# Attention and two mixture layers on one core: gate logits cut into queued pieces, and second products of the small experts without a summing product

## Chip, core and metric

The kernel runs on one core of a Trainium2 chip. TensorE multiplies matrices into PSUM; VectorE (DVE), ScalarE (ACT) and GpSimd (POOL) do the element-wise work; SyncE (SP) issues most of the transfers. The metric is the device time of one execution in microseconds (us). All data is 32-bit floating point; TensorE takes it as pairs of words (`float32r`, high and low part, three products for one) up to the first expert, and as plain `float32` in the small experts, where one product of the program is two matmul records of the trace.

## The reference

```python
def reference(q, k, v, w_in, w_out, w_skip, w_gate, w1, w2):
    x = block_causal_attention(q, k, v)          # 4 x 8 heads x 576 x 64 -> 2304 tokens x 512
    h = x @ w_in                                 # 512 -> 2048
    x = np.maximum(0.01 * h, h) @ w_out          # leaky maximum, 2048 -> 512
    do_compute = x @ w_skip > 0                  # tokens that go to an expert
    xc = x[do_compute]
    logits = xc @ w_gate                         # 8 experts
    e_idx, gate_w = argmax(logits), softmax(logits)[argmax]
    for e in range(8):
        m = e_idx == e
        y[m] = gate_w[m] * (relu(xc[m] @ w1[e]) @ w2[e])     # 512 -> 1024 -> 512
    out = x; out[do_compute] = xc + y
```

## The kernel before

The program is traced in Python; a scheduler fixes the order of the instructions on every engine at build time. It takes an instruction when its inputs are ready by its own reckoning, earlier traced ones first. `tc.keep_in_program_order` (`pin`) holds an instruction of an engine to the traced order. `tc.issue_after(ins)` makes the instructions traced inside it that run on the engine of `ins` come after `ins` in that engine's queue.

**Attention** and a quarter of the leaky layer take the first 315 us. **The main loop** (L1088 to L1123) does the rest of the leaky layer: 384 tokens `n` at a time, 72 passes `i`, in each a first product `b_mm1` (12 matmuls of 384 columns into `ph`, one of two PSUM banks) and, for the pass two earlier, a second product `b_mm2` (9 matmuls of 512 columns into `acc`). Between the two stands `leaky`: ACT scales `ph` into `u`, DVE takes the maximum of `ph` and `u` (L517), ACT casts it to `gh`, POOL subtracts to `gl` (L518). The bank of `ph` is free when DVE's maximum has read it. Tokens come in the order 3, 4, 5 (four inner blocks each, three times over), then 0, 1, 2 (twelve each). When the last block of an `n` is summed, L902 adds three times on DVE, and the routing steps of this `n` go into a list `rq` from which each pass takes one, from pass 60 on two. They are `keep` (stores), three of `logits` (one for 128 tokens), `route`, `place_all` (the row of each token in the lists) and `put` (three indirect transfers from POOL's queue, L847). For `n` = 3, 4, 5 and 0, `logits` multiplies on DVE: for each of nine rows `wrow` one instruction multiplies 128 x 512 numbers and sums them (L748), and a short one reads the sum. For `n` = 1 the logits are TensorE's (`logits_last`); 2 comes behind the loop. In pass 67 the lists are read back (`load_lists(lf)`, L713), and `gather(first)` (L717) fetches the first expert's tokens; after pass 71 TensorE turns them (`turn_x`, L989).

**The sorted experts** come last. Expert 0's tiles run at full precision; the other seven experts are sorted by their count of tokens, and the tail (L1427 to L1445) computes seven units: three `Groups` units of 96 tokens, two of 32, a `Half` of 64 and a `Full` of 128, the last two for one expert. A unit has `first` and `rest` (first product and ReLU on ACT), `turn` (transposes, then a DVE copy into `hT`, L1275), `second` (second product) and `end`. In pass `i` of the tail TensorE's pinned order is `first` of the next unit, `turn`, `rest` of the next, `end` of the one before, `turn_x` two units on, `second`. A group of `m` = 32 tokens fills a quarter of TensorE's columns, so four products with their own weights run side by side and write four quarters of a bank `pp`: in `second_product` (L1277) each quarter takes another quarter of the 1024 inner rows, so the bank holds four partial sums of one 32 x 512 result. ACT or DVE copies the bank to `ev` (L1394, for `Half` L1358), and `end` multiplies `ev` with `sums`, a matrix of ones that adds the quarters (L1399; `Half`, with two halves, L1362). `end_tile` multiplies by the gate and adds the input on DVE (L1291) and scatters the rows (L1292). Weights arrive expert by expert from `load_rank` on SP's queue, each into the place of one that is done.

Of the kernel before, what the change touches and what calls it, by code (L numbers as in the profile page):

```python
# [10 lines left out]
F32 = mybir.dt.float32  # L11
# [5 lines left out]
ALU = mybir.AluOpType  # L17
AX = mybir.AxisListType
# [379 lines left out]
def attention_moe_kernel(  # L398
# [13 lines left out]
    nc = tc.nc  # L412
    B, H, S, HD = q.shape
    NT, D = out.shape
# [6 lines left out]
    E, _, F2 = w1.shape  # L421
    ND = D // 128
    NF2 = F2 // 128
    TB = 3
# [7 lines left out]
    ident = C.tile([128, 128], F32, name="ident")  # L432
# [6 lines left out]
    CV = ctx.enter_context(tc.tile_pool(name="cv", bufs=2))  # L439
# [192 lines left out]
    psx = ctx.enter_context(tc.tile_pool(name="psx", bufs=1, space=PSUM))  # L632
# [51 lines left out]
    def load_rows():  # L684

        for j, nm in ((0, "raw"), (2, "raw"), (4, "raw"), (6, "cv2"), (7, "cv2"), (8, "cv2")):
            n = 2 if nm == "raw" else 1
            t = CV.tile([128, n, D], F32, name=nm, bufs=3)
            nc.sync.dma_start(t, wr_d[j : j + n].unsqueeze(0).to_broadcast([128, n, D]))
            wrow.extend(t[:, k_] for k_ in range(n))  # L690
# [34 lines left out]
    def routing_steps(n, x2):  # L725
        box = {}
        last, late = n == order[-1], n in order[-2:]
# [3 lines left out]
        pin = tc.keep_in_program_order if last else lambda ins: ins  # L731
# [7 lines left out]
                nc.sync.dma_start(x2_d[pos * 128 : (pos + TB) * 128].rearrange("(t p) d -> p t d", p=128), x2)  # L739
            tc.keep_in_program_order(nc.sync.dma_start(out[rows].rearrange("(t p) d -> p t d", p=128), x2))  # L740

        def logits(t):

            if t == 0:
                box["L"] = s3("lg", 1 + E)
            for j in range(1 + E):
                junk = M2.tile([128, D], F32, name="xlast", bufs=3)
                nc.vector.tensor_tensor_reduce(out=junk, in0=x2[:, t], in1=wrow[j], scale=1.0, scalar=0.0,  # L748
                                               op0=ALU.mult, op1=ALU.add, accum_out=box["L"][:, t, j : j + 1])
# [100 lines left out]

        if last:
            return dict(keep=keep, turn=turn_last, mul=mul_last, route=route, rank=rank, place=place_all, put=put)
        return [keep] + [lambda t=t: (logits_last if late else logits)(t) for t in range(TB)] + [route, place_all, put]

    parts = {}

# [18 lines left out]
    def b_mm1(n, f):  # L875
        if f == 0 and n not in parts:
            load_part(n)
        ph = ps2.tile([128, 512], F32, name="ph2", bufs=2)[:, 0:BT]
        o = (n % 3) * BT
        three(ph, [(wi_b[0](c, f), wi_b[1](c, f)) for c in range(ND)],  # L880
              [(xT[0][:, c, o : o + BT], xT[1][:, c, o : o + BT]) for c in range(ND)], True, True)
        gh = M2.tile([128, BT], F32R, name="gh", bufs=2)
        gl = M2.tile([128, BT], F32R, name="gl", bufs=2)
        ends = leaky(M2, ph, BT, gh, gl, 2)
        gq[n, f] = (gh, gl)
        if f == NFB - 1 and n >= 3:
            load_x(n - 3)
        return ends
# [198 lines left out]
    rq = []  # L1087
    for i in range(len(seq) + lag):  # L1088
        gate[:] = ends if i else a_ends
        if wb and i % 3 < 2:  # L1090
            wb.pop(0)()
            if not wb:
                gate.clear()
                load_rows()
        if i < len(seq):
            ends = b_mm1(*seq[i])
        for _ in range(1 if i < len(seq) - NFB else 2):
            if rq:
                rq.pop(0)()
        f = i - (len(seq) - NFB)  # L1100
        if f == 3:
            for j in range(AHEAD):
                if tags[j]:
                    load_piece(j)
        if 4 <= f < 8:
            run_all(w_steps(f - 3))
        if f == 7:

            load_lists(lf, lambda l: l[0:256, :].rearrange("(n p) c -> p n c", p=128), nc.sync)
            find(lf, 0, 1)  # L1110
            gather(first, NT - BT)
        if f == NFB - 1:
            with ExitStack() as behind:
                for ins in ends:
                    behind.enter_context(tc.issue_after(ins.ins))
                run_all(w_steps(8))
        if i >= lag:
            n, f = seq[i - lag]
            add = b_mm2(n, f)
            if f == NFB - 1 and n != order[-1]:  # L1120
                rq += routing_steps(n, parts[n])
        if i == len(seq):
            turn_x(first, psx.tile([128, ND, 128], F32, name="py", bufs=1), False)  # L1123
# [27 lines left out]
    MG, MH = 32, 64  # L1151
# [44 lines left out]
    _, rank = nc.values_load_multi_w_load_instructions(tab[0:1, 0:NR, 0], engines=[mybir.EngineType.SP], min_val=1, max_val=NR)  # L1196
# [46 lines left out]
    M3 = ctx.enter_context(tc.tile_pool(name="m3", bufs=2))  # L1243
# [6 lines left out]
    pin = tc.keep_in_program_order  # L1250
    bank = lambda nm: ps3.tile([128, 512], F32, name=nm, tag="ps")
# [24 lines left out]

    def second_product(pp, w, h, m):  # L1277

        s = 128 // m
        n = NF2 // s  # L1280
        for i in range(n):
            for j in range(s):
                pin(nc.tensor.matmul(pp[j * m : j * m + m], h[:, i * 128 + j * m : i * 128 + j * m + m], w[1][j * n + i], start=(i == 0), stop=(i == n - 1)))  # L1283

    def end_tile(y, lx, n=128):
        yo = M3.tile([128, 512], F32, name="yo")
        y = y if isinstance(y, list) else [y]
        w = D // len(y)
        for k_, t in enumerate(y):
            c = slice(k_ * w, k_ * w + w)  # L1290
            nc.vector.scalar_tensor_tensor(out=yo[0:n, c], in0=t[0:n], scalar=lx["li"][0:n, 2:3], in1=lx["xg"][0:n, c], op0=ALU.mult, op1=ALU.add)  # L1291
        nc.gpsimd.indirect_dma_start(out=out[:, :], out_offset=bass.IndirectOffsetOnAxis(ap=lx["ix"][0:n, 1:2], axis=0),  # L1292
                                     in_=yo[0:n], in_offset=None, bounds_check=NT - 1, oob_is_err=False)

# [19 lines left out]
    class Full(Unit):  # L1314
# [17 lines left out]
        def second(self):  # L1332
            self.y = [bank("py")[:, 0:256] for _ in range(2)]
            for k_ in range(2):
                for f in range(NF2):
                    pin(nc.tensor.matmul(self.y[k_], hT[:, f // 4, f % 4 * 128 : f % 4 * 128 + 128], self.w[1][f][:, k_ * 256 : k_ * 256 + 256],
                                         start=(f == 0), stop=(f == NF2 - 1)))

        def end(self):
            end_tile(self.y, self.lx, self.n)  # L1340

    class Half(Unit):

# [11 lines left out]
        def second(self):  # L1355
            pp = bank("pp")
            second_product(pp, self.w, hT[:, 0], MH)
            nc.scalar.copy(ev[0], pp)  # L1358

        def end(self):  # L1360
            y = psx.tile([128, 512], F32, name="py", bufs=1)
            pin(nc.tensor.matmul(y[0:MH], sums[MH], ev[0], start=True, stop=True))  # L1362
            end_tile(y, self.lx, MH)

    class Groups(Unit):

# [21 lines left out]
                turn_groups(h2[a // 2], hT[:, a // 2], 2 * min(2, self.n // MG - a))  # L1388

        def second(self):  # L1390
            for g in range(self.n // MG):
                pp = bank("pp")
                second_product(pp, self.w, hT[:, g // 2, g % 2 * 256 : g % 2 * 256 + 256], MG)
                (nc.vector.tensor_copy if g % 2 else nc.scalar.copy)(ev[g], pp)  # L1394

        def end(self):
            y = psx.tile([128, 512], F32, name="py", bufs=1)
            for g in range(self.n // MG):
                pin(nc.tensor.matmul(y[g * MG : g * MG + MG], sums[MG], ev[g], start=True, stop=True))  # L1399
            end_tile(y, self.lx, self.n)  # L1400

    units = [Groups(r - 1, r, r, CAPS[r]) for r in range(1, 6)] + [Half(5, 0, NR, MH), Full(6, 0, 0, 128)]
    U = len(units)
# [13 lines left out]
        held[r] = load_rank(r)  # L1417

    h2 = [CV.tile([128, 512], F32, name="cv3", bufs=3) for _ in range(2)]
    hT, ev01, ev23 = (CV.tile([128, 2, 512], F32, name="raw", bufs=3) for _ in range(3))  # L1420
    ev = [ev01[:, 0], ev01[:, 1], ev23[:, 0], ev23[:, 1]]
    hx = CV.tile([128, 512], F32, name="cv2", bufs=3)
    sums = {m: M3.tile([128, m], F32, name=f"sum{m}", bufs=1) for m in (MG, MH)}
    for m, t in sums.items():
        nc.vector.reduce_sum(out=t, in_=ident.rearrange("p (s t) -> p t s", t=m), axis=AX.X)

    units[0].first()  # L1427
    units[0].rest()
# [26 lines left out]
    lx = lane32(llate, 0, xgs[4], xws[2])  # L1455
    to = held[places_of[3]]
    w = split(to)

    def half(row):
        load_lists(part, lambda l: l[bass.ds(row, MH), :].unsqueeze(1), nc.sync)  # L1460
        find(part)
        gather_n(lx, MH)
        turn_n(lx, MH)
        ph = bank("ph3")
        first_product(ph, w, lx["xw"][:, :, 0:MH], MH)
        relu(hx, ph)
        turn_groups(hx, hT[:, 1])
        pp = bank("pp")
        second_product(pp, w, hT[:, 1], MH)
        nc.scalar.copy(hx, pp)  # L1470
        y = bank("py")
        pin(nc.tensor.matmul(y[0:MH], sums[MH], hx, start=True, stop=True))
        end_tile(y, lx, MH)

    with tc.If(spill > 0):
        with tc.For_i(0, E, 1) as r:
# [36 lines left out]
```

## Time and profile before

| | us |
|---|---|
| three runs | 764.28, 765.04, 766.53 |
| median | 765.04 |
| the profiled execution | 765.64 |
| its span, first to last instruction | 763.8 |
| TensorE busy in it | 730.6 (96%) |
| DVE, ACT, POOL busy | 460.4, 354.9, 319.2 |
| mean granted clock of TensorE | 0.994 of 2.4 GHz |

Times in the rows are microseconds from the start of the span, unless they are marked ns; the profiled execution is 1.84 us longer than its span. A busy TensorE is not TensorE at its peak. L12 is line 12 of the kernel; names are those of its tiles, without numbers. PEld is TensorE's loading of weights, SPq and POOLq the queues of engines that issue transfers.

### The profile page before, as it was taken

To read this page: it belongs to the slowest core of one execution; us is meant where nothing else is said; L and a number is where in the kernel's file an instruction comes from. 1 tells how busy PE (TensorE), PEld (TensorE's weight loads), DVE (VectorE), ACT (ScalarE), POOL (GpSimd) and SP (SyncE) were. 2 spreads that over 40 slices of the span, in tenths; PEclk is the share of its full clock that TensorE was granted. 3 is DMA by queue.
4 is the path that set the end of the run, shared out by engine and by line. 5 is a ranking of instruction groups with operands and counts; after the bars stand their busy time and mean duration, and the time that the engine had idled before them with its cause. 6 is when DMAs were issued, how large, how long until landed. Compare 5 with 4: busy or idle time off the path is not lost.

```text
span 763.8 us, 12641 instructions
## 1 busy us (share of the span) xinstructions
PE 730.6 (96%) x4454; PEld 593.1 (78%) x4455; DVE 460.4 (60%) x1067; ACT 354.9 (46%) x824; POOL 319.2 (42%) x429
## 2 busy tenths in 40 slices
PE   5999899999999999999999999999999998999995
PEld 4666778788888788899999998879899976875333
DVE  5888887764668646666773499988821365221211
ACT  4786887775788746555452222222223251222110
POOL 4656683454335436454442342545431543210111
PEclk9999999999999999999999999999999999999998
DMA  8545644522330214732223457112302221999900
GB/s 183 136 116 133 181 103 113 144 65 73 90 77 17 95 58 148 272 100 81 98 83 111 123 150 251 56 43 84 125 0 83 57 96 32 301 399 397 353 25 24
DMA packets 101109, 96.92 MB, mean 127 GB/s; under 512 B 69198, under 2 KB 72270, under 8 KB 101042
## 3 DMA queue, kind: packets, MB, share of 16 engines
q1 hardware_dynamic: 92578, 82.28, 34.5%
q0 software_dynamic: 7264, 13.50, 6.1%
q8 instruction: 36, 0.59, 0.3%
q10 hardware_dynamic: 1200, 0.30, 0.2%
q14 instruction: 31, 0.25, 0.1%
HBM read 74.38 MB, written 21.98 MB: 126 GB/s over the span
## 4 chain that ended last, share of the span: by engine, by line
PE 64%; DVE 21%; ACT 7%; DMA 3%; issue 2%; POOL 1%; SPq 0%; POOLq 0%; ACTq 0%; DVEq 0%
PE ph L526 18%; PE acc L526 12%; DVE xlast L748 9%; PE pv L345 4%; PE po L526 3%; PE ph L1269 3%; PE pp L1283 3%; PE pt L288 3%; PE py L1004 2%; PE sp L229 2%; PE ph L1004 2%; ACT P L193 2%; PE sp L182 2%; DVE stat L192 2%; PE big L110 1%
## 5 line engine op out<-in xcount | busy, mean ns | idle before, releaser
L526 PE MATMUL ph<-xT,wbt 128*128 128x384 f32 x864 | 167.2, 338 | 3.9 <-DVE u L517 2.1
L526 PEld LDWEIGHTS ph<-xT,wbt 128*128 128x128 f32 x864 | 151.8, 188 | 13.5 <-DVE u L517 3.9
L518 POOL TENSOR_TENSOR gl<-u,gh 128x384 fp32r<-128x384 f32 x72 | 80.5, 1119 | 144.5 <-ACT gh L517 140.8
L526 PE MATMUL acc<-wbt,gh 128*128 128x512 f32 x432 | 132.2, 393 | 0.0
L201 POOL TENSOR_SCALAR P<-P,stat 128x256 f32<-128x256 f32 (+4 forms) x144 | 80.0, 573 | 89.5 <-DVE stat L199 73.3
L517 ACT CAST gh<-u 128x384 fp32r<-128x384 f32 x72 | 37.0, 514 | 121.2 <-DVE u L517 49.6
L526 PEld LDWEIGHTS acc<-wbt,gh 128*128 128x128 f32 x432 | 79.7, 188 | 12.0
L517 DVE TENSOR_TENSOR u<-ph,u 128x384 f32<-128x384 f32 x72 | 39.7, 551 | 71.4 <-ACT u L516 71.3
L526 PE MATMUL acc<-wbt,gl 128*128 128x512 f32 x216 | 82.2, 395 | 0.0
L516 ACT ACTIVATE u<-ph 128x384 f32<-128x384 f32 x72 | 35.3, 490 | 61.3 <-PE ph L526 58.2
L288 PE MATMUL pt<-ident,P 128*128 128x128 f32 x400 | 58.2, 275 | 4.4 <-ACT P L193 1.8
L192 DVE TENSOR_REDUCE stat<-sp 128x1 f32<-128x384 f32 (+7 forms) x88 | 45.9, 527 | 25.1 <-PE sp L229 12.8
L288 PEld LDWEIGHTS pt<-ident,P 128*128 128x128 f32 x400 | 47.0, 140 | 16.5 <-ACT P L193 5.4
L193 ACT ACTIVATE P<-sp,stat 128x384 f32<-128x384 f32 (+7 forms) x88 | 49.8, 567 | 20.2 <-DVE stat L192 18.6
L526 PE MATMUL ph<-xT,wia 128*128 128x384 f32 x288 | 57.6, 344 | 0.6 <-ACT xT L350 0.5
L473 POOL TENSOR_TENSOR cv<-cv,cv 128x512 int32<-128x512 int32 x32 | 43.7, 1366 | 33.7 <-DVE cv L472 26.9
L526 PE MATMUL po<-woa,gA 128*128 128x512 f32 x216 | 55.4, 399 | 0.0
L748 DVE CUSTOM_DVE_ANT_0 xlast<-x,raw 128x512 f32<-128x512 f32 x72 | 55.1, 804 | 0.0
L526 PEld LDWEIGHTS ph<-xT,wia 128*128 128x128 f32 x288 | 49.4, 188 | 2.3 <-ACT xT L350 0.7
L345 PE MATMUL pv<-ph,vn 128*64 128x320 f32 (+4 forms) x448 | 49.6, 370 | 0.4 <-ACT P L242 0.3
L526 PEld LDWEIGHTS acc<-wbt,gl 128*128 128x128 f32 x216 | 40.4, 188 | 8.5
L345 PEld LDWEIGHTS pv<-ph,vn 128*64 128x64 f32 x448 | 30.3, 140 | 20.8 <-issue 2.8
(282 smaller groups left out, 1249.6 us busy)
## 6 DMA issues: line engine op xcount, KB each, us to landing
wbt<-in_moe_w_dram SPq DMA_DIRECT2D x40, 512.0 KB
raw<-in_moe_w_in_dram SPq DMA_DIRECT2D x16, 512.0 KB
raw<-in_moe_w_out_dram SPq DMA_DIRECT2D x16, 512.0 KB
xTd<-xT POOLq DMA_DIRECT2D x4, 1152.0 KB
part_d<-cv SPq DMA_DIRECT2D x18, 256.0 KB
x<-part_d SPq DMA_DIRECT2D x6, 768.0 KB
xT<-xTd POOLq DMA_DIRECT2D x6, 768.0 KB
out_dram<-x SPq DMA_DIRECT2D x6, 768.0 KB
```

The lines of the kernel that those rows point to most:

```text
L192: self.recent["max"] = nc.vector.tensor_reduce(out=st_[:, 1, i : i + 1], in_=sv, op=ALU.max, axis=ax, negate=True)
L193: self.recent["exp"] = nc.scalar.activation(out=P, in_=sv, func=AF.Exp, bias=st_[:, 1, i : i + 1], accum_out=st_[:, 0, i : i + 1])
L201: nc.gpsimd.tensor_scalar(out=P, in0=P, scalar1=rs[:, i : i + 1], scalar2=1.0, op0=ALU.mult, op1=ALU.mult)
L288: nc.tensor.transpose(o, src, self.ident)
L345: self.pin(nc.tensor.matmul(box["pv"][64 * h : 64 * h + 64, c0:N], st()["vs"][:, jc, h], box["ph"][:, i, h, cs], start=(jc == 0), stop=(jc ...
L473: nc.gpsimd.tensor_tensor(out=w, in0=w, in1=low, op=ALU.add)
L516: nc.scalar.activation(out=u, in_=ph, func=AF.Copy, scale=0.01)
L517: return [nc.vector.tensor_tensor(out=u, in0=ph, in1=u, op=ALU.max), nc.scalar.copy(gh, u), nc.gpsimd.tensor_tensor(out=gl, in0=u, in1=gh. ...
L518: nc.gpsimd.tensor_tensor(out=gl, in0=u, in1=gh.bitcast(F32), op=ALU.subtract)]
L526: nc.tensor.matmul(ps, x, y, start=first and m == 0, stop=last and m == 3 * n - 1)
L748: nc.vector.tensor_tensor_reduce(out=junk, in0=x2[:, t], in1=wrow[j], scale=1.0, scalar=0.0, op0=ALU.mult, op1=ALU.add, accum_out=box["L"] ...
L1004: nc.tensor.matmul(ps, x, y, start=(i == 0), stop=(i == len(l) - 1))) for i, (x, y) in enumerate(l)]
```

## The change

Two edits. In the main loop, the logits of 128 tokens are two steps of `rq` (five rows of `wrow`, then four); `keep` is no step of its own for these `n` but opens the first piece, so seven steps become nine; and every step's instructions on DVE are queued behind the leaky maximum of the same pass. In the tail, a group's four quarters take other work: two of them the left 256 columns of the result, two the right, each over half of the inner rows (with `m` = 64: one half of the columns each, over all rows). DVE multiplies each quarter by the gate and adds it to the output tile straight from PSUM (`add_groups`), in `second`; the copies to `ev`, the products with ones, `ev` and `sums` go, and `end` only scatters. The same edit is made in a path for spilled tokens.

```diff
-        def logits(t):
-            if t == 0:
+        def logits(t, js):
+            if t == 0 and js[0] == 0:
+                keep()
                 box["L"] = s3("lg", 1 + E)
-            for j in range(1 + E):
+            for j in js:
...
-        return [keep] + [lambda t=t: (logits_last if late else logits)(t) for t in range(TB)] + [route, place_all, put]
+        if late:
+            turns = [keep] + [lambda t=t: logits_last(t) for t in range(TB)]
+        else:
+            turns = [lambda t=t, js=js: logits(t, js) for t in range(TB) for js in (range(0, 5), range(5, 1 + E))]
+        return turns + [route, place_all, put]
...
             if rq:
-                rq.pop(0)()
+                with tc.issue_after(ends[0].ins):
+                    rq.pop(0)()
...
     def second_product(pp, w, h, m):
         s = 128 // m
         n = NF2 // s
-        for i in range(n):
+        for i in range(2 * NF2 // s):
             for j in range(s):
-                pin(nc.tensor.matmul(pp[j * m : j * m + m], h[:, i * 128 + j * m : i * 128 + j * m + m], w[1][j * n + i], start=(i == 0), stop=(i == n - 1)))
-
-    def end_tile(y, lx, n=128):
-        yo = M3.tile([128, 512], F32, name="yo")
-        y = y if isinstance(y, list) else [y]
-        w = D // len(y)
-        for k_, t in enumerate(y):
-            c = slice(k_ * w, k_ * w + w)
-            nc.vector.scalar_tensor_tensor(out=yo[0:n, c], in0=t[0:n], scalar=lx["li"][0:n, 2:3], in1=lx["xg"][0:n, c], op0=ALU.mult, op1=ALU.add)
+                f = j // 2 * 4 + i
+                c, d = f % n * 128 + f // n * m, j % 2 * 256
+                pin(nc.tensor.matmul(pp[j * m : j * m + m, 0:256], h[:, c : c + m], w[1][f][:, d : d + 256], start=(i == 0), stop=(i == 2 * NF2 // s - 1)))
+
+    def add_groups(yo, pp, lx, t0, m):
+        r = slice(t0, t0 + m)
+        for j in range(128 // m):
+            c = slice(j % 2 * 256, j % 2 * 256 + 256)
+            nc.vector.scalar_tensor_tensor(out=yo[r, c], in0=pp[j * m : j * m + m, 0:256], scalar=lx["li"][r, 2:3], in1=(lx["xg"], yo)[j // 2][r, c], op0=ALU.mult, op1=ALU.add)
...
     class Half(Unit):
...
             second_product(pp, self.w, hT[:, 0], MH)
-            nc.scalar.copy(ev[0], pp)
+            self.yo = out_tile()
+            add_groups(self.yo, pp, self.lx, 0, MH)
 
         def end(self):
-            y = psx.tile([128, 512], F32, name="py", bufs=1)
-            pin(nc.tensor.matmul(y[0:MH], sums[MH], ev[0], start=True, stop=True))
-            end_tile(y, self.lx, MH)
+            end_tile(self.yo, self.lx, MH)
 
     class Groups(Unit):
...
         def second(self):
+            self.yo = out_tile()
             for g in range(self.n // MG):
                 pp = bank("pp")
                 second_product(pp, self.w, hT[:, g // 2, g % 2 * 256 : g % 2 * 256 + 256], MG)
-                (nc.vector.tensor_copy if g % 2 else nc.scalar.copy)(ev[g], pp)
+                add_groups(self.yo, pp, self.lx, g * MG, MG)
 
         def end(self):
-            y = psx.tile([128, 512], F32, name="py", bufs=1)
-            for g in range(self.n // MG):
-                pin(nc.tensor.matmul(y[g * MG : g * MG + MG], sums[MG], ev[g], start=True, stop=True))
-            end_tile(y, self.lx, self.n)
+            end_tile(self.yo, self.lx, self.n)
...
-    hT, ev01, ev23 = (CV.tile([128, 2, 512], F32, name="raw", bufs=3) for _ in range(3))
-    ev = [ev01[:, 0], ev01[:, 1], ev23[:, 0], ev23[:, 1]]
+    hT = CV.tile([128, 2, 512], F32, name="raw", bufs=3)
     hx = CV.tile([128, 512], F32, name="cv2", bufs=3)
-    sums = {m: M3.tile([128, m], F32, name=f"sum{m}", bufs=1) for m in (MG, MH)}
-    for m, t in sums.items():
-        nc.vector.reduce_sum(out=t, in_=ident.rearrange("p (s t) -> p t s", t=m), axis=AX.X)
```

## Rows read from the trace of the kernel before

**Rows 1.** Chain that ended last, main loop: start, us, what.

```profile
424.35 2.08 PE ph L526 x12
426.43 2.08 PE acc L526 x9
```

**Rows 2.** Windows: length, busy PE, PEld, DVE, ACT, POOL; clock, DMA share, GB/s.

```profile
432.60:549.36 116.76, 114.19 (x599) 101.23 (x598) 109.73 (x325) 26.12 (x58) 48.39 (x49) 1.00 0.38 122
499.32:507.66 8.34, 7.07 (x34) 5.57 (x32) 8.34 (x27) 0.91 (x2) 1.64 (x2) 1.00 0.00 0
```

**Rows 3.** Groups by line, 428 to 552 us: busy, mean ns | idle before, releaser.

```profile
L526 PE MATMUL ph<-xT,wbt 128*128 128x384 f32 x345 | 66.9, 339 | 2.5 <-DVE u L517 2.1 <-issue 0.4
...
L748 DVE CUSTOM_DVE_ANT_0 xlast<-x,raw 128x512 f32<-128x512 f32 x72 | 55.1, 804 | 0.0
...
L748 DVE CUSTOM_DVE_ANT_0 xlast<-x,cv 128x512 f32<-128x512 f32 x36 | 25.2, 723 | 0.0
...
L517 DVE TENSOR_TENSOR u<-ph,u 128x384 f32<-128x384 f32 x28 | 15.3, 546 | 6.6 <-ACT u L516 6.6
```

**Rows 4.** Timeline of DVE, two neighbouring logits.

```profile
444.35 0.68 DVE L748 CUSTOM_DVE_ANT_0 xlast<-x,raw 128x512 f32<-128x512 f32 x1
...
444.96 0.68 DVE L748 CUSTOM_DVE_ANT_0 xlast<-x,raw 128x512 f32<-128x512 f32 x1
```

**Rows 5.** Timeline from the lists to the first expert's turned tokens.

```profile
609.69 1.03 POOL L717 DMA_INDIRECT xgf<-x_d,lfix  x1 [1.10 <-DVE lfix L708]
...
617.32 0.27 PE L989 MATMUL py<-ident,xgf 128*128 128x128 f32 x1
...
623.10 0.68 DVE L995 TENSOR_TENSOR xtf<-py,xtf 128x512 fp32r<-128x512 f32 x1
```

**Rows 6.** Chain that ended last: a gather's wait, then the tail.

```profile
638.28 3.27 DMA xgf<-x_d,lfix
...
690.46 3.59 PE ph L1269 x64
...
707.15 5.29 PE pp L1283 x48
712.44 0.86 PE ph L1269 x16
713.30 0.81 PE pt L1274 x6
714.11 1.00 PE ph L1269 x16
715.11 0.85 PE py L1399 x6
715.96 0.36 PE pt L1259 x4
...
741.96 0.98 PE py L1399 x2
742.93 3.58 PE pp L1283 x16
746.52 1.02 PE pt L1274 x8
747.54 1.00 PE py L1362 x2
748.54 7.12 PE py L1336 x32
```

**Rows 7.** Groups by line and form, 676 to 764 us.

```profile
L1291 DVE SCALAR_TENSOR_TENSOR yo<-py,rankli,xg 128x256 f32<-128x256 f32 x2 | 1.0, 484 | 5.9 <-PE py L1336 5.9
...
L1291 DVE SCALAR_TENSOR_TENSOR yo<-py,rankli,xg 32x512 f32<-32x512 f32 x1 | 0.7, 737 | 3.7 <-PE py L1399 3.7
```

**Rows 8.** Timeline of DVE in the tail: copies into `hT`.

```profile
713.93 1.02 DVE L1275 COPY raw<-pt 128x512 f32<-128x512 f32 x2 [2.44 <-PE pt L1274]
...
747.14 1.29 DVE L1275 COPY raw<-pt 128x512 f32<-128x512 f32 x2 [3.43 <-PE pt L1274]
```

More of the change, by code (lines that the diff above doesn't have):

```diff
@@ L1280, in second_product, with end_tile @@
         n = NF2 // s
-        for i in range(n):
+        for i in range(2 * NF2 // s):
             for j in range(s):
-                pin(nc.tensor.matmul(pp[j * m : j * m + m], h[:, i * 128 + j * m : i * 128 + j * m + m], w[1][j * n + i], start=(i == 0), stop=(i == n - 1)))
-    def end_tile(y, lx, n=128):
-        yo = M3.tile([128, 512], F32, name="yo")
-        y = y if isinstance(y, list) else [y]
-        w = D // len(y)
-        for k_, t in enumerate(y):
-            c = slice(k_ * w, k_ * w + w)
-            nc.vector.scalar_tensor_tensor(out=yo[0:n, c], in0=t[0:n], scalar=lx["li"][0:n, 2:3], in1=lx["xg"][0:n, c], op0=ALU.mult, op1=ALU.add)
+                f = j // 2 * 4 + i
[6 more added lines that the diff above has]
+            nc.vector.scalar_tensor_tensor(out=yo[r, c], in0=pp[j * m : j * m + m, 0:256], scalar=lx["li"][r, 2:3], in1=(lx["xg"], yo)[j // 2][r, c], op0=ALU.mult, op1=ALU.add)
+    out_tile = lambda: M3.tile([128, 512], F32, name="yo")
+    def end_tile(yo, lx, n=128):
         nc.gpsimd.indirect_dma_start(out=out[:, :], out_offset=bass.IndirectOffsetOnAxis(ap=lx["ix"][0:n, 1:2], axis=0),
@@ L1339, in end @@
         def end(self):
-            end_tile(self.y, self.lx, self.n)
+            yo, lx = out_tile(), self.lx
+            for k_, y in enumerate(self.y):
+                c = slice(k_ * 256, k_ * 256 + 256)
+                nc.vector.scalar_tensor_tensor(out=yo[:, c], in0=y, scalar=lx["li"][:, 2:3], in1=lx["xg"][:, c], op0=ALU.mult, op1=ALU.add)
+            end_tile(yo, lx)
     class Half(Unit):
@@ L1469, in half @@
         second_product(pp, w, hT[:, 1], MH)
[L1470 to L1473, printed above, removed]
+        yo = out_tile()
+        add_groups(yo, pp, lx, 0, MH)
+        end_tile(yo, lx, MH)
     with tc.If(spill > 0):
```

## The prediction

> **What bounds the kernel now.** I read the page first. TensorE is busy nearly throughout, so a change pays where it takes work off TensorE or ends one of its few stalls. The chain of work that ended last says where that is. In the main loop it is nothing but passes of two equal parts, 12 matmuls of `b_mm1` in 2.08 us and 9 of `b_mm2` in 2.08: 4.16 us a pass [rows 1]. In the tail it is TensorE's records without a gap, up to the last product [rows 6]; no transfer and no other engine stands in it. So the tail's length is the sum of TensorE's records.
>
> For the stretch of the logits I took windows. From 432.6 to 549.4 us, 28 passes, DVE is busy 109.7 of 116.8 us and TensorE 114.2: it idles 2.57 us, half of it (1.27) in one window in which DVE never rests [rows 2]. The groups by line name the reason: `b_mm1` waited 2.5 us, 2.1 of it for DVE's maximum in `u` [rows 3]. That is all the main loop can give.
>
> **The logits in pieces.** One of the 108 logits comes 0.61 us after the other [rows 4]. Their mean busy times of 804 and 723 ns against 680 of an undisturbed one [rows 3, 4] add (0.124 x 72 + 0.043 x 36) = 10.5 us of stretching over 28 passes, 0.4 a pass. A pass with nine logits therefore asks of DVE 9 x 0.61 + 0.55 (the maximum [rows 3]) + 0.4 = 6.4 us and lasts 4.16. The bank of `ph` is wanted again three parts later, after 6.25 us; less ACT's and DVE's half microsecond each, a maximum may come some 5.1 us late. Nine logits in front of it (5.5 to 5.9 us) are too many by under a microsecond, which is the size of the stalls.
>
> After the change a pass asks 5 x 0.61 + 0.55 + 0.4 = 4.0 us or 4 x 0.61 + 0.95 = 3.4: both fit a pass, and no maximum stands behind more than five logits. Nine steps for seven spread the work of `n` = 3, 4, 5, 0 over passes 30 to 62 instead of 30 to 57: DVE's 109.7 us and five more maxima, 112.5, in 137 us, 82% against 94%. The logits are not shortened; their cover is the passes that follow, in which DVE has room.
>
> Two places can take some back. From pass 60 two steps are popped a pass, so pass 60 gets nine logits again, and 61 four and the routing: DVE is 2.3 us late after the one and, by my estimate, 3.5 after the other, inside 5.1, but the order on its queue may put a maximum last. And `n` = 1 starts one pass later, so `put`, POOL's three indirect transfers, the lists on SP's queue and `gather(first)` behind them move by 4.16 us. That gather was issued at 609.69; one like it took 3.27 us, so it landed near 612.96, and TensorE turned its tokens at 617.32 [rows 5, 6]: 4.36 us of room, 0.2 of it left. If it is late, the next link is DVE's `xtf`, which began only at 623.10 behind other work [rows 5], so the first microsecond or so is still hidden. `keep`, now in the first piece, puts its stores on SP's queue in the same pass as before for `n` = 3; behind them stand loads that are wanted passes later. I take a gain of the 2.57 us less 0.5: **2.0**, with bounds of 2.6 gained and 2 lost.
>
> **The second products.** Removed from TensorE: three sums of 0.85 us (one is shown), two of 0.98, one of 1.00 [rows 6]: 5.51 us, all on the chain.
>
> Added: matmuls half as wide and twice as many. The narrow form stands in the same trace, in the first products: 64 records of 256 columns in 3.59 us, 56.1 ns each; 48 of 512 columns took 5.29, 110.2 each [rows 6]. A group's second product goes from 16 x 110.2 = 1.76 us to 32 x 56.1 = 1.80. Shorter runs of the narrow form took 0.86 and 1.00 us for 16 [rows 6], 53.8 to 62.5 ns, which bounds a group between 1.72 and 2.00. I take the long run, being the same form at the same length: 11 groups x 0.03 = 0.4 us lost (bounds 0.4 gained, 2.6 lost). `Half`'s 3.58 us becomes 32 records, two side by side; at 7.12 / 32 for a 256-column record [rows 6] that is 3.56: nothing.
>
> The Trainium skill speaks against this part: "TensorE: Matmul & The Clock Gate", section "Wait — 56ns, not 53.3ns?", has the sequencer spend some 62 ns on a matmul when hardware decode is off, and bind where the array needs less. By it the 352 narrow records would take 21.8 us instead of 19.7, and the sum would be 2.1 us worse. The 56.1 ns of the long run lie under that figure.
>
> Moved to DVE: 46 adds of 256 columns instead of copies on ACT and DVE and six wide adds. A 256-column add took 0.484 us; 32 rows save nothing against 128 (0.737 for 32 x 512) [rows 7]. Neighbours on DVE can overlap by 0.07, as logits of 0.68 us do that come 0.61 apart [rows 4]. Four adds of a group so take between 1.73 and 1.94 us, beside TensorE's 1.80: DVE just keeps up and ends some 2 us behind TensorE. Queued behind them are the copies into `hT` for the next unit. The tightest place is the first 32-token neighbour: after a second product TensorE has 0.86 + 0.81 + 1.00 + 0.36 = 3.03 us of other records before the next one [rows 6], and the sum of 0.85 no longer pads it. DVE needs about 2.0 for adds and 1.02 for the copies [rows 8]: 3.0. I price a wait of 0.15 in all (bounds 0 and 0.4). Without those pads the copies are next in line.
>
> Under the last sum the cover goes for certain. `Full`'s second product began 2.02 us after `Half`'s ended: 1.02 of transposes and 1.00 of sum [rows 6], and the copies ended at 748.43 [rows 8], just before. Now `Half`'s two adds (0.9 us) stand before the copies (1.29), so the product starts 1.5 to 2.3 us after `Half`'s. I take 2.0: that 1.00 is not won (bounds 0.5 won, 0.3 lost). ACT's copies and the making of `sums` were beside TensorE's work and cost nothing before or after.
>
> Sum of this part: 5.51 - 0.4 - 1.0 - 0.15 = **4.0 us** gained, bounds 1.2 and 5.5.
>
> **Sum.** The profiled execution took 765.64 us; 765.64 - 2.0 - 4.0 = 759.6. The median of the runs lies 0.6 below it, so I forecast **759.0**.
>
> **Rivals.**
> *The stalls stay* (0.12): the order on DVE's queue is fixed at build time, and the stalls move to passes 60 to 62 or to the adds L902 instead of ending. For it: DVE is still 82% busy. Time: 765.0 - 4.0 = 761.0.
> *DVE sets the tail's pace* (0.12): if a 256-column add costs what a 512-column one does, 0.737, a 96-token unit asks 12 x 0.737 + 1.02 = 9.9 us of DVE, and TensorE's round there, 9.17 from second product to second product [rows 6], is 8.3 without the sum. Two such rounds lose 1.5 each: 762.1. It begins at 0.61 an add. Against it: the 0.484. "TensorEngine Tiling" of the Trainium skill, section on the PSUM bottleneck, warns of this very thing and wants both ScalarE and VectorE to empty PSUM; the change leaves it to VectorE.
> *Narrow records at 62.5 ns* (0.05): 11 groups lose 0.24 instead of 0.03: 761.3. Against it: the run of 64.
> *The first gather is two passes late* (0.05): 8.3 - 4.36 = 4.0 us of waiting at 617: 763.0, no change that can be told.
> *Slower* (0.06): the third and fourth add of a group read what the first and second wrote, and all of them read one quarter of the partitions and may write another, which no row shows. If each waits for the one before and costs two, 0.97, a round asks 12.7 us against 8.3: 8.8 lost in the two rounds, 767.8. It decides from 0.95 an add.
>
> **How the numbers follow.** The forecast has 0.60, with a range of its own from 757.4 to 761.0. I call 0.3% (2.3 us, so 762.7) what a measurement can tell. Faster: 0.60 + 0.12 + 0.12 + 0.05, less 0.04 for those whose spread reaches over 762.7: 0.85. Within: 0.04 + 0.05 = 0.09. Slower: 0.06. The range takes in the first three rivals and, below, both parts near their upper bounds: 756.8 to 762.8; it leaves out the last two and some 0.05 at the lower end.
>
> **What would show it.** Right: no wait of `b_mm1` for `u` between 432 and 550 us and at most 0.5 near passes 60 to 62; TensorE turning the first expert's tokens some 2 us earlier than 617.3; runs of 32 narrow records in 1.8 us; adds at 0.47 to 0.49 us; the stretch from the second unit's second product (707.15) to the last unit's (748.54 [rows 6]) shorter by about 3 us, two of the 0.85 and both of the 0.98 less 0.4. Wrong: TensorE's weight loads waiting for copies into `hT`, adds over 0.6 us, a wait for the gather before `turn_x`, or new waits for L902 in the main loop.

## The result and the profile after

| kernel | runs | median us | range | ratio to before, 95% interval |
|---|---|---|---|---|
| before | 6 | 764.43 | 764.10 to 766.53 | |
| changed | 6 | 757.26 | 756.91 to 759.46 | 0.9907 [0.9891, 0.9922] |

The change makes the kernel faster by 7.2 us, 0.9%, where the forecast had 6.0; the median lies 1.7 us below the forecast of 759.0, part of it because the median of before is 0.6 lower with all six runs. The profiled execution of the changed kernel took 757.12 us, against 765.64 before: 8.5 us. The working below is held against this pair.

The chain by engine, on the pages of before and of after:

```profile
PE 64%; DVE 21%; ACT 7%; DMA 3%; issue 2%; POOL 1%; SPq 0%; POOLq 0%; ACTq 0%; DVEq 0%
```

```profile
PE 76%; DVE 10%; ACT 8%; DMA 3%; issue 2%; POOL 1%; SPq 0%; POOLq 0%; ACTq 0%; DVEq 0%
```

DVE gave up 11 points of the chain. The logits are 9 of them: `xlast`, what they write, was 9% before and is not among the fifteen lines that the page names after.

**Main loop.** The two windows of [rows 2], after:

```profile
432.60:549.36 116.76, 116.76 (x613) 105.33 (x611) 89.76 (x256) 28.23 (x59) 49.62 (x50) 1.00 0.32 102
499.32:507.66 8.34, 8.34 (x52) 7.44 (x51) 3.26 (x15) 1.97 (x5) 3.52 (x4) 1.00 0.27 93
```

TensorE never idles and gets through 613 records in the time of 599. DVE's work in the window fell from 109.7 to 89.8 us. The groups by line, 428 to 552 us, which answer to [rows 3]:

```profile
L526 PE MATMUL ph<-xT,wbt 128*128 128x384 f32 x360 | 68.8, 337 | 0.0
...
L749 DVE CUSTOM_DVE_ANT_0 xlast<-x,raw 128x512 f32<-128x512 f32 x58 | 41.6, 768 | 0.0
L749 DVE CUSTOM_DVE_ANT_0 xlast<-x,cv 128x512 f32<-128x512 f32 x27 | 24.6, 954 | 0.0
```

The wait for `u` is gone, and only 85 logits of 108 are in the stretch: the others come later. TensorE's waits by cause, 425 to 620 us, hold one row. Before has this wait as well, with the same 1.4, but later, at 624.43 us and so outside this window (its add is L902 there):

```profile
PE rt L759 <- DVE x L907: 1.4, 1, 1.4
```

How much was won, the chain tells. Its rows below are the loop's first products (at 311 us, not at 315) and ACT's last cast, which the second product of the last pass releases; first the chain of before, then that of after.

```profile
310.98 4.43 PE ph L526 x24
...
617.29 0.51 ACT gh L517
```

```profile
310.60 4.45 PE ph L526 x24
...
612.76 0.51 ACT gh L517
```

From the first of these rows to the start of the second the loop took 306.31 us before and 302.16 after: it is 4.15 us shorter, not 2.0. The cast comes 4.53 earlier, but 0.38 of that stood already at the loop's first record, before anything that the change touches. POOL's timeline has the gather, and TensorE's the first turned token (one kernel, two views):

```profile
605.81 1.02 POOL L717 DMA_INDIRECT xgf<-x_d,lfix  x1 [2.23 <-DVE lfix L708]
```

```profile
612.79 0.27 PE L994 MATMUL py<-ident,xgf 128*128 128x128 f32 x1
```

From issue to use there are now 6.98 us, against 7.63 before [rows 5]: of the room, 0.65 us is gone, not 4.16.

**Tail.** The chain of after, parts that answer to [rows 6]:

```profile
677.65 7.04 PE ph L1275 x128
...
689.57 5.32 PE pp L1292 x96
...
703.30 0.47 DVE yo L1298
703.77 0.03 issue
703.81 0.48 DVE yo L1298
...
708.92 0.49 DVE yo L1298
709.41 0.03 issue
709.44 0.70 DVE raw L1281
710.14 0.04 issue
710.19 5.43 PE pp L1292 x96
...
718.19 0.44 DVE raw L1281
718.62 0.04 issue
718.67 1.93 PE pp L1292 x32
...
734.66 3.60 PE pp L1292 x32
738.26 1.04 PE pt L1280 x8
739.30 0.02 issue
739.32 0.70 DVE raw L1281
740.02 0.04 issue
740.06 7.19 PE py L1347 x32
```

The sums are gone, but TensorE is no longer alone on the chain: twelve adds, each beginning as the one before ends, lead to a copy into `hT` and so to the second product at 710.19. The same happens at 718.67. Before the last product the chain names the transposes (`pt`), which end at 739.30; two adds end there too, so that both copies come behind them. The waits by cause, 677 to 764 us (us in total, times, longest), put numbers to it; before, this view is empty:

```profile
PE pp L1292 <- DVE raw L1281: 0.9, 2, 0.5
PE py L1347 <- DVE raw L1281: 0.8, 1, 0.8
```

The adds by form, 676 to 764 us, beside the 484 and 737 ns of [rows 7]:

```profile
L1298 DVE SCALAR_TENSOR_TENSOR yo<-pp,rankli,yo 32x256 f32<-32x256 f32 x22 | 10.6, 483 | 0.7
L1298 DVE SCALAR_TENSOR_TENSOR yo<-pp,rankli,xg 32x256 f32<-32x256 f32 x20 | 9.5, 475 | 6.7 <-PE pp L1292 6.2
```

The last unit's product starts at 740.06, 8.48 earlier than before: 0.38 of it stood before the loop, 4.15 come from the loop and 3.95 from what follows, the tail.

### The profile page after: what moved, and what is told of

Its sections match the earlier page's. It is cut to its first block, busy times and chain, and to the rows that moved or that the text cites. A ratio compares the mean times of both kernels' runs of the same rounds, so it can differ in the third digit from the quotient of the medians.

```text
span 755.4 us, 12990 instructions
## 1 busy us (share of the span) xinstructions
PE 723.2 (96%) x4622; PEld 597.5 (79%) x4623; DVE 476.2 (63%) x1102; ACT 350.8 (46%) x815; POOL 320.5 (42%) x429
## 4 chain that ended last, share of the span: by engine, by line
PE 76%; DVE 10%; ACT 8%; DMA 3%; issue 2%; POOL 1%; SPq 0%; POOLq 0%; ACTq 0%; DVEq 0%
PE ph L526 24%; PE acc L526 19%; PE pv L345 4%; PE po L526 3%; PE pt L288 3%; PE pp L1292 3%; PE ph L1275 3%; PE py L1009 2%; PE ph L1009 2%; PE sp L229 2%; ACT P L193 2%; PE sp L182 2%; DVE stat L192 2%; PE big L110 1%; ACT wbt L134 1%
## 5 line engine op out<-in xcount | busy, mean ns | idle before, releaser
L526 PE MATMUL ph<-xT,wbt 128*128 128x384 f32 x864 | 165.5, 337 | 1.2 <-ACT cv L574 1.2
L518 POOL TENSOR_TENSOR gl<-u,gh 128x384 fp32r<-128x384 f32 x72 | 83.1, 1157 | 136.9 <-ACT gh L517 124.8
L749 DVE CUSTOM_DVE_ANT_0 xlast<-x,raw 128x512 f32<-128x512 f32 x72 | 51.6, 765 | 0.0
## 6 DMA issues: line engine op xcount, KB each, us to landing
wbt<-in_moe_w_dram SPq DMA_DIRECT2D x40, 512.0 KB, 11.4
```

The lines of the kernel that those rows point to most:

```text
L518: nc.gpsimd.tensor_tensor(out=gl, in0=u, in1=gh.bitcast(F32), op=ALU.subtract)]
L526: nc.tensor.matmul(ps, x, y, start=first and m == 0, stop=last and m == 3 * n - 1)
```

## Experiments

Each table row beside the diffs gives the median of the runs and the ratio to before with its interval; the first table also has the loop, from the start of its first record to that of ACT's last cast (before 310.98 to 617.29: 306.31; after 310.60 to 612.76: 302.16). Over all thirteen profiled executions the loop's first record starts anywhere from 309.6 to 311.5 us, so its length is compared and not its end. Kernels of one table ran on one chip, beside the same runs of before.

**The two parts alone.** One kernel has the diff's main-loop part and the old tail, one the new tail and the old main loop.

> The main loop's part alone, the tail as before. Counted from start to start of TensorE's records, the kernel before loses 4.4 us between 432 and 550 us and the changed one 0.1; the busy times of the windows gave 2.57. Theory (the spacing is the true loss): 764.4 - 4.4 = 760.0, with the last product of the main loop some 4.4 us earlier. Rival (the windows are right and the rest of the profile's difference is chance): 761.9.

> The tail's part alone, the main loop as before. Theory: 5.5 us of sums go, 1.9 us of new waits for DVE's copies come, 0.1 for narrow records: 764.4 - 3.5 = 760.9. Rival (the tail gives what the main loop does not, 7.2 - 2.6): 759.8. The waits should stand before the second products of the third and fourth unit (0.5 each) and before the last unit's (0.85).

**The main-loop part, split.** One kernel cuts the logits in pieces but doesn't queue them, the other queues whole steps; both have the old tail.

```diff
# pieces, not queued
-                with tc.issue_after(ends[0].ins):
-                    rq.pop(0)()
+                rq.pop(0)()
# whole steps, queued: logits(t) and the list of steps as before the change, and
-                rq.pop(0)()
+                with tc.issue_after(ends[0].ins):
+                    rq.pop(0)()
```

> The logits in two pieces each (nine steps), but not queued behind the leaky maximum; tail as before. If the stalls end because the same work of DVE is spread over nine passes instead of seven, this is as fast as the main loop's part whole: 760.0 to 760.5. If the place in DVE's queue ends them, most stalls stay: 762 to 764.

> Whole logits (seven steps as before), each step queued behind the leaky maximum of its pass; tail as before. If spreading is the cause, DVE is as full as before and the time stays at 763.5 to 766, or worse by up to 2 us, since nine logits now stand together. If the place in the queue is the cause: 760 to 761.5.

| before 765.18 (17 runs) | runs | median us | ratio | loop |
|---|---|---|---|---|
| main-loop part alone | 5 | 761.96 | 0.9953 [0.9940, 0.9965] | 310.38 to 612.59: 302.21 |
| tail alone | 5 | 761.93 | 0.9949 [0.9936, 0.9961] | 311.35 to 617.62: 306.27 |
| pieces, not queued | 12 | 764.94 | 1.0000 [0.9988, 1.0012] | 310.14 to 616.37: 306.23 |
| whole steps, queued | 5 | 761.98 | 0.9953 [0.9940, 0.9966] | 311.19 to 614.15: 302.96 |

Both parts pay, each about half. The medians alone do not decide between the expectations of the two parts: 761.96 is the figure of the rival and not the theory's 760.0, but before ran 0.75 slower here than in the first comparison, and against it the gain of 2.7 to 4.6 us takes in the theory's 4.4 and only just leaves out 2.57. The loop's length decides: 4.1 us shorter than before. The tail alone, with a gain of 3.0 to 4.9 us, fits both figures that were expected of it; its trace, from the tail's first record to the last unit's product, has 62.41 us, and the three kernels with the old tail in this table 65.94 each, with the same first product: 3.53 us, the theory's 3.5.

In the main loop it is the queueing that pays: pieces without it win nothing that can be measured, whole steps with it as much as the edit by the runs and 3.35 of its 4.1 to 4.15 us by the loop's length. `b_mm1`'s waits between 425 and 620 us, first with pieces unqueued, then with whole steps queued:

```profile
PE ph L526 <- DVE u L517: 2.0, 4, 0.7
```

```profile
PE ph L526 <- DVE u L517: 0.7, 1, 0.7
```

Why pieces alone do nothing stands in DVE's order, here decoded from the traces: the start of each maximum and what follows it (x a logit, its short read left out, X one of over 0.75 us, A one of the three adds that sum an `n`, r other routing).

```
pieces, not queued                changed kernel
445.37 xxXxxxr                    447.72 xxxAAxA
450.39 AxAXAxrx                   452.43 xxxx
455.38 xr                         455.34 xxxXX
456.53 rrrxxXrrxxxrrx             460.49 rrrrrrr
463.24 xxrrxxxx                   464.20 rrArArArrrrrrr
468.35 AxAXAxrx                   468.70
473.36 xxrrx                      472.89 xxxxx
476.64 xxrrxxxrx                  477.06 xxxX
481.82 xrrrrrrxxXrrx              481.22 xxxXx
487.06 xxrrxrrxxrr                485.56 xxxX
491.75 xxXxx                      489.56 xxxXx
496.06 xxXxxx                     494.00 xxXx
501.02 xxrxxxrx                   497.89 rrrrrrr
506.14 xrrrrrrrrrrrrrrr           502.06 rrrrrrrrrrr
```

On the left, the logits for `n` = 4 begin in the row of 456.53, at 457.8 us, as soon as its blocks are summed (A, from 450.39) and those of `n` = 3 are done; queued, they begin at 473.4, nearly four passes later, and keep to five or four a pass. The scheduler does not care in which pass a step was traced: it takes a step as soon as its inputs are there, and so two groups of logits follow each other without a rest, with maxima 4.8 us apart from 463.2 to 506.1 (nine steps in 42.9) where TensorE's pass takes 4.16. Once the slack of the bank is used up, TensorE goes at DVE's pace. `issue_after` is what ties a step to its pass.

**More logits a pass.** The changed kernel with pieces of seven rows for five and four; five of the nine rows are multiplied twice, with the same result, and nothing is left out.

```diff
-            turns = [lambda t=t, js=js: logits(t, js) for t in range(TB) for js in (range(0, 5), range(5, 1 + E))]
+            turns = [lambda t=t, js=js: logits(t, js) for t in range(TB) for js in ((0, 1, 2, 3, 4, 0, 1), (5, 6, 7, 8, 5, 6, 7))]
```

> The changed kernel with pieces of seven rows and seven (five of the nine rows are multiplied twice, with the same result), queued as before: a dose of more DVE work in the same places. Theory (DVE's pace against TensorE's 4.17 us a pass, with about 5 us that a maximum may be late): a pass asks 7 x 0.61 + 0.95 = 5.2 us, six such passes are 6.3 late, adds L907 on top: stalls of 1 to 3 us for each of four token groups come back, 761 to 769. Rival (only the place in the queue counts, the amount does not): 757.3 within 1.

**The copies elsewhere.** The changed kernel with the copies into `hT` on ScalarE.

```diff
-        nc.vector.tensor_copy(dst[:, 0 : n * 128], pt[:, 0 : n * 128])
+        nc.scalar.copy(dst[:, 0 : n * 128], pt[:, 0 : n * 128])
```

> The changed kernel with the copies into hT on ACT instead of DVE, so that they do not stand behind the adds. Theory: the waits of 0.54, 0.54 and 0.85 us before three second products are DVE's queue, and go: 757.3 - 1.9 = 755.4. Rival (the products wait for the transposes and their copy anyway, ACT's copy being as late): 757.3 within 0.5.

**Twice the work for DVE.** The changed kernel with the old second product (16 records of 512 columns for 32 tokens, four partial sums in the bank), each partial sum added by DVE at its full width. Nothing is left out: the sums are still not products.

```diff
         for j in range(128 // m):
-            c = slice(j % 2 * 256, j % 2 * 256 + 256)
-            nc.vector.scalar_tensor_tensor(out=yo[r, c], in0=pp[j * m : j * m + m, 0:256], scalar=lx["li"][r, 2:3], in1=(lx["xg"], yo)[j // 2][r, c], op0=ALU.mult, op1=ALU.add)
+            nc.vector.scalar_tensor_tensor(out=yo[r], in0=pp[j * m : j * m + m], scalar=lx["li"][r, 2:3], in1=(yo if j else lx["xg"])[r], op0=ALU.mult, op1=ALU.add)
```

> The changed kernel with the quarters of the old second product (512 columns, four partial sums a group) and four adds of 512 columns straight from PSUM: twice the columns for DVE, no sums on TensorE either. Theory (DVE sets the pace once a round of 12 adds and copies passes TensorE's 8.3 us): adds 0.77 apart ask 12 x 0.77 + 1.0 = 10.3, two rounds lose 2 each against 0.54 now, and the units of 32 and 64 about 1 each: 761 to 763. Rival (DVE's time is hidden beside TensorE): 757.3 within 1.

The changed kernel itself ran beside them:

> The changed kernel once more, beside the others on one chip: 757.3 within 0.7, or 0.990 to 0.991 of the kernel before; waits in the tail as in its first profile.

| before 765.52 (11 runs) | runs | median us | ratio |
|---|---|---|---|
| seven rows a piece | 5 | 769.25 | 1.0045 [1.0032, 1.0058] |
| copies on ScalarE | 6 | 756.52 | 0.9891 [0.9871, 0.9911] |
| wide adds | 4 | 758.59 | 0.9903 [0.9888, 0.9917] |
| changed kernel again | 5 | 759.80 | 0.9930 [0.9917, 0.9943] |

The changed kernel missed its own expectation: one of its five runs, 756.69, had a mean granted clock of 0.995, the other four, 759.73 to 761.51, of 0.988 to 0.992 (the last section has more on this). So 759.80 is no measure for its neighbours, and the copies on ScalarE, 1.1 us above the 755.4 that was expected, were run again beside it (below).

Seven rows a piece, queued like the others, bring the stalls back and more. The waits, 425 to 620 us:

```profile
PE ph L526 <- DVE u L517: 5.4, 5, 1.8
PE acc L526 <- POOL gl L518: 0.6, 2, 0.3
```

By [rows 3, 4] DVE is asked for 7 x 0.61 + 0.55 = 4.8 us a pass, where a pass has 4.16, and TensorE follows: the loop, from 310.55 to 624.07 us, takes 313.52, 11.4 more than in the changed kernel. About 1.5 of that belong to a stretch of low clock in this execution (granted clock 0.57 from 580 to 584 us); the rest are stalls. So the queue alone is not enough; what is tied to a pass must fit it.

The wide adds missed what was expected of them. They cost about what a 512-column add cost before (737 ns [rows 7]), by form, 676 to 764 us:

```profile
L1295 DVE SCALAR_TENSOR_TENSOR yo<-pp,rankli,yo 32x512 f32<-32x512 f32 x33 | 24.7, 748 | 1.1
```

Yet TensorE's waits in the tail are no longer than with narrow adds (0.9 and 0.8 there):

```profile
PE pp L1290 <- DVE raw L1281: 1.3, 2, 0.7
PE py L1344 <- DVE raw L1281: 0.4, 1, 0.4
```

DVE's timeline shows why: the scheduler puts the copy ahead of adds that are left over, and these run on beside TensorE's next products.

```profile
711.30 0.75 DVE L1295 SCALAR_TENSOR_TENSOR yo<-pp,rankli,yo 32x512 f32<-32x512 f32 x1
712.08 1.02 DVE L1281 COPY raw<-pt 128x512 f32<-128x512 f32 x2
713.13 1.53 DVE L1295 SCALAR_TENSOR_TENSOR yo<-pp,rankli,yo 32x512 f32<-32x512 f32 x2
```

**Both, and a repeat.** The copies on ScalarE once more, the wide adds with these copies, and the changed kernel.

> The changed kernel with the copies into hT on ScalarE, once more, beside the changed kernel itself on the same chip. If the copies' place behind VectorE's adds costs what the trace of the changed kernel and the first run of this edit show (0.54, 0.54 and 0.48 us of waits that go away): 1.2 to 1.6 us below the changed kernel run beside it, about 756.0 where that one is 757.3. If ScalarE's copies are later at other places, or the waits only move: the same within 0.5 us.

> The wide form (four adds of 512 columns for 32 tokens, quarters of F as before) with the copies into hT on ScalarE. If VectorE's lateness at the copies is all that its adds cost, the wide form loses its three waits (0.80, 0.66 and about 0.5 us) and is no slower than the narrow form with the same copies: within 0.5 us of it. If VectorE's 12 us of adds for 128 tokens set a pace of their own (banks of the second product not free in time, the chunk's turn for the next unit late behind them), it is 1.5 to 4 us slower than the narrow form, with waits of TensorE for the adds or for the turned inputs.

> The changed kernel itself, as the measure for the two beside it. Expected 756.7 to 759.9, the spread of its runs so far, with a median near 757.5.

| before 765.20 (9 runs) | runs | median us | ratio | tail's first record to last unit's product |
|---|---|---|---|---|
| copies on ScalarE | 5 | 756.27 | 0.9883 [0.9866, 0.9900] | 678.64 to 739.49: 60.85 |
| wide adds, copies on ScalarE | 5 | 755.92 | 0.9881 [0.9865, 0.9898] | 680.14 to 740.87: 60.73 |
| changed kernel | 4 | 757.14 | 0.9891 [0.9876, 0.9907] | 678.52 to 740.93: 62.41 |

With the copies on ScalarE one wait is left in the tail, the same for narrow and wide adds. The two kernels have this row each:

```profile
PE py L1347 <- ACT raw L1281: 0.3, 1, 0.3
```

```profile
PE py L1344 <- ACT raw L1281: 0.3, 1, 0.3
```

The tail is 1.6 us shorter (62.41 - 60.85) by the traces. The medians say 0.9 and 1.2, with intervals that overlap the changed kernel's, so the runs alone don't prove it; the waits that vanish do show where it comes from. The first run of the same edit agrees: 61.37 there, with a first product of unit 0 that took 0.52 longer. Splitting the result in two halves of columns is worth nothing here once the copies are off DVE (0.9883 against 0.9881): the tail's gain is the missing sums.

## Why the prediction was right in sign and short in size

**"That is all the main loop can give" failed, in size.** The idle time of 2.57 us [rows 2] was taken for the whole loss. The chain spoke against it. The prediction found in the main loop's chain "nothing but passes of two equal parts", which holds for the two rows that it shows, from before the first logits; from 424 to 552 us more than half of the chain was DVE's logits:

```profile
by line: DVE xlast L748 56.1%; PE ph L526 10.0%; DVE u L517 8.1%; PE acc L526 6.9%; DVE x L902 5.1%; issue 3.3%; DVE go L785 1.5%; DVE oh L787 1.5%; DVE lg L748 0.9%; DVE ohb L789 0.9%; DVE nt L821 0.8%; ACT u L516 0.8%; DVE cb L824 0.8%; D
```

From the start of one TensorE record to that of the next, the same stretch before lost 0.9 (432 to 480 us), 3.1 (480 to 520) and 0.4 (to 549), 4.4 in all; after, 0.1. A record is shown busy for 0.34 to 0.40 us while the next may start 0.174 or 0.232 after it. So the first 0.17 us of a stall lies under the record before it: four stalls of 0.79, 0.53, 0.94 and 0.84 us are shown as 0.62, 0.36, 0.77 and 0.67 idle, and those below 0.17 not at all. The loop's length, 4.15 us less, agrees. Of the 2.5 us by which the difference of the two profiled executions exceeds the forecast, 2.15 are this term (4.15 for 2.0) and 0.38 stood before the loop. The Trainium skill, "Perfetto Trace Analysis", at its head and in "Identifying the Most-Contended Engine", calls matmul busy time a bad measure of how close a kernel is to roofline, because matmuls are pipelined. Here the same pipelining hid 1.8 us of a loss of 4.4.

**"Nine steps for seven spread the work" failed, in cause.** The steps spread nothing: unqueued pieces run as before (1.0000 [0.9988, 1.0012]), queued whole steps win 0.9953. That a spread is what ends the stalls was right (DVE 89.8 us in the window, not 109.7), but it is `issue_after` that makes it, by holding each step to its pass. With the pieces the last 0.8 us of stall goes too, which the medians (761.96, 761.98) can't tell. "No maximum behind more than five logits" holds in the trace up to 561 us, but whole steps, with six to eight between some maxima, do as well in the runs; by these orders what decides is whether DVE gets a rest, as seven rows a piece (1.0045) show. Nor did the stalls of before come from nine logits in front of one maximum, as the prediction priced them: decoded in the same way, its trace has at most seven between two maxima. They came from a run of logits that asked 4.8 us of DVE for each pass and never paused.

**Passes 60 to 62 and the gather.** The 0.5 us set aside for them was not lost: no stall of over 0.15 us start to start stands between 432 and 612 us. The lists were not four microseconds late either, as "`n` = 1 starts one pass later" had it. The gather lost 0.65 us of its room. Why it lost so little was not tried.

**The second products: size right, two terms off in opposite ways.** The sums gave what they were priced at: they took 5.87 us start to start, 0.33 of which the neighbouring records gave back, 5.54 for a forecast of 5.51. Narrow records cost less: 96 take 5.20 us from their first start to the next record's, 54 ns each, where 48 wide ones took 5.17; 0.03 per 96 tokens, not 0.1, and a rival at 62.5 ns fell. The figure of some 62 ns in "TensorE: Matmul & The Clock Gate", "Wait — 56ns, not 53.3ns?", of the Trainium skill did not bind here either: it holds where decode is not in hardware, and no run here shows which way this one decodes. New waits of TensorE for the copies into `hT`, which the prediction had named as a sign of being wrong, cost more, 0.54 + 0.54 + 0.85 us, against 0.15 for copies and the 1.00 of `Half`'s sum not won. Unit 0's first product took 7.04 us, not 7.49, which makes up for it; other executions of the same tail have 7.59, so that is no gain of the change. The sum by these terms is 5.54 - 0.1 - 1.93 + 0.45 = 4.0, as measured and as forecast. That it meets the forecast so well is luck: the waits were 0.78 above their price, the records 0.3 below, and the 0.45 is not the change's. Between executions with the same first product the tail is 3.53 us shorter.

**"Neighbours on DVE can overlap by 0.07" failed.** Adds of 0.475 to 0.483 us come 0.51 apart, with 0.02 to 0.03 between them, while TensorE takes 1.73 us for a group's second product. Four adds take 2.04 us. The slower rival had 0.97 for an add that waits for the one before. It fell too: an add that reads what an earlier one of its group wrote starts 0.03 us after the end of its neighbour, and so does one that reads nothing of its group's; a wide add, which reads what the add right before it wrote, comes 0.78 after that one's start, again with a gap of 0.03.

**"DVE sets the tail's pace" fell even at its own price.** The rival wanted 0.737 an add and gave 762.1. The wide adds cost 0.748, and from the tail's first record to the last unit's product that kernel took 62.87 us (679.53 to 742.40), 0.55 of it by a slower first product of unit 0, against 62.41: no loss where the rival had 3. The step that failed is that DVE must finish a round's adds before the next copy: the scheduler places the copy ahead of leftover adds, which run beside TensorE's next products. What costs is not DVE's total but what stands ahead of a copy. "TensorEngine Tiling (Array Packing)" of the Trainium skill, "PSUM Bottleneck", wants PSUM emptied by both ScalarE and VectorE; here this is right, by 1.6 us in the trace, for the copies alone.

The other rivals: stalls that stay, and the gather two passes late, did not come.

## What to carry to other kernels

Before pricing a stall by idle time, take start to start of the engine's records: busy time of pipelined matmuls hides the first part of each stall. A scheduler that places instructions when inputs are ready undoes a spread that was only written in the trace order; tie the work to its pass, and check that what is tied fits. When work moves to an engine that also makes the next stage's input, look at what order it takes: a small copy behind a train of adds can cost more than the adds, as it did here.

## What the runs showed of the hardware

The granted clock fell to half in stretches of about 3.4 us. One near 92 us stands in twelve of the thirteen profiled executions; the others come at places that change from run to run. With the wide adds one lay near 626 us, where the changed kernel kept its full clock (length, busy PE, PEld, DVE, ACT, POOL; clock, DMA share, GB/s); the two kernels, one row each:

```profile
626.00:630.00 4.00, 4.00 (x19) 3.02 (x20) 1.73 (x13) 0.22 (x1) 0.00 (x0) 0.57 0.02 8
```

```profile
626.00:630.00 4.00, 4.00 (x27) 2.90 (x27) 2.94 (x19) 1.30 (x3) 0.00 (x0) 1.00 0.02 6
```

Of 2.4 and 1.2 GHz, the mean of 0.57 is nearly all the lower level, while TensorE is busy throughout. In the six us before, it was busy 5.75 of 6.00 in the one and 6.00 of 6.00 in the other. From the start of ACT's last cast in the loop to the tail's first record the four executions with such a stretch there took 66.33 (seven rows a piece), 66.42, 66.45 and 66.49 us, the others 64.87 to 64.96: about 1.5 us a stretch. The spread between runs of one kernel goes with the clock. Of the changed kernel's fifteen runs the ten with a mean granted clock of 0.995 took 756.69 to 757.99 us, the five at 0.988 to 0.992 took 759.46 to 761.51. That it is such stretches in those five is not shown, since none of them was profiled.
